# Moving attention side work between the units of a fused attention, rational-MLP and SoLU kernel

## The chip, the cores and the metric

The kernel runs on one core of one Trainium2 chip. The metric is the device time of one execution in microseconds (us), as the median of several runs. A profile is one further execution, recorded by the hardware profiler, with its own time.

## The reference

Three stages follow each other on 4 sequences of 768 tokens, with 8 heads of 48 (model width 384). What the kernel computes, cut to the core:

```python
# attention: a gated linear recurrence, state 48 x 48 for each head
state = alpha[:, :, t, :, None] * state + einsum('bhd,bhe->bhde', k[:, :, t], v[:, :, t])
y[:, :, t] = einsum('bhd,bhde->bhe', q[:, :, t], state)
x = y as (3072 tokens, 384)
# first feed-forward, 384 -> 2048 -> 384, a rational function in between
h = x @ w_in
g = (a[0] + a[1] * h + a[2] * h**2 + a[3] * h**3) / (1 + |b[0]| * |h| + |b[1]| * h**2 + 1e-6)
x = g @ w_out
# second feed-forward, 384 -> 1024 -> 384
h = x @ w_in2
ln = layer_norm(h * softmax(h)) * g_ln
out = ln @ w_out2
```

The weights come in 64-bit words that are turned into float32 on the chip. Float32 products are made of three passes with operands split into a high and a low part (hi x hi, hi x lo, lo x hi).

## The kernel before

**Units and halves.** The 3072 tokens are cut into 6 chunks of 512, and the first feed-forward runs in 96 units: unit u works on chunk u // 16 and on columns 128 (u % 16) of the hidden layer. A unit has an up-projection `m_up` of 9 matmuls of 512 columns (L592) into one of three PSUM banks "h", and a chain of elementwise steps: on ScalarE abs L597, two squares L599 and L600, ln L619, exp L620 and the rounded high part gh L625; on VectorE L618, L621, L622, L623; on GpSimd the low part gl L626. The down-projection `m_down` of 9 matmuls (L638) follows four units later and adds up over a chunk's 16 units in three PSUM banks x2p. There is one set of these banks, so the first down-projection of a chunk waits until the copies of the last sums (x2e, L646 on ScalarE) have left them; SP then stores x2e (L647).

**Side work.** Eight units are a half, and beside each half runs the attention of one half chunk ahead (`half_steps`, L853): two generators are advanced by a step a unit. `a_pe` makes the scores in two parts (L420 on TensorE, copy L427 on ScalarE, causal mask L428 on GpSimd), then y (L444; high part L470 on ScalarE, low part L471 on VectorE), then the keys-values product u (L483; state updated on VectorE L493 and GpSimd L494). The preparation `a_dve` (transposes L290 to L337, the scan L317) runs for the half after, then moves of q and k, loads of alpha and k (L266) for the half after that, and at the end `a_enter`. Scores, y, u and the conversions below share a ring of two PSUM banks "at".

**Second weights.** The 14 tiles of the second feed-forward's weights are converted by `split_w` as side work, two tiles a half: load L533 into a buffer "st", three integer steps on VectorE (L537, L540, L541), a scale L546 (tiles of the second matrix alone) and a rounding copy L547 on ScalarE, a subtraction on GpSimd (L548), a store L550. The tag "st" has two buffers, which x2e and the output tiles o use too.

**Second phase.** From unit 80 the last chunk runs, and from unit 89 the second feed-forward's tiles of 128 tokens begin, 24 in all: `n_up` (18 matmuls, L712), softmax and norm `n_soft`, `n_norm` (L731 to L752), every four tiles a turn `n_turn` by 16 SP transfers (L762), `n_split` into high part (L767, ScalarE) and low part (L768, GpSimd, tiles 0 and 20 VectorE), `n_down` (24 matmuls, L776, two banks "op") and `n_out` (copy L785 on ScalarE, four stores L788 on SP). `SKIP` names the tiles s after which no `n_down` follows, so that as many are left for the tail behind the last `n_up`.

**What sets the order.** The program is written in the order of this loop; a list scheduler of the framework then orders each engine's instructions by its own costs, and `issue_after` keeps some of them behind a named instruction. On each engine and DMA queue instructions start in that order. Buffers of a ring are handed on when their last reader is done.

Of the kernel before, what the change touches and what calls it, by code (L numbers as in the profile page):

```python
# [30 lines left out]
def kernel(  # L31
# [17 lines left out]
    B, H, S, D = q.shape  # L49
# [7 lines left out]
    NF1 = DF1 // 128  # L57
# [20 lines left out]
    G2 = 3  # L78
    MIX = lambda u: u < 24 and u % 2 == 0
    EARLY = (9, 11, 13, 15)  # L80
    SKIP = (5, 7, 11)
    AHEAD = 3
    LATE = 2
    U2, IDLE = NF1 - 1, (0, NF1 // 2 - 1)
    assert (B, H, D, CH) == (4, 8, 48, 128)

    const = ctx.enter_context(tc.tile_pool(name="const", bufs=1, side="left"))
# [65 lines left out]
    def network(fast):  # L153
# [257 lines left out]
        def a_pe(i):  # L411
# [4 lines left out]
            for p in range(2):  # L416
                sc = [ps_ap.tile([128, B, CH], F32, name="sc", tag="at") for j in range(2)]
                for x in range(B):
                    for j in range(2):
                        nc.tensor.matmul(  # L420
                            sc[j][:, x, :],
                            lhsT=hf.k[p][64 * j:64 * j + D, x, :], rhs=hf.q[p][64 * j:64 * j + D, x, :],
                            start=True, stop=True,
                        )
                for j in range(2):
                    t = A[p, j] = ap_.tile([128, B, CH], F32, name="A", tag=f"A{p}{j}")
                    nc.scalar.activation(t, sc[j], AF.Copy)  # L427
                    nc.gpsimd.affine_select(  # L428
                        out=t, in_=t, pattern=[[0, B], [1, CH]], compare_op=ALU.is_ge, fill=0.0, base=0,
                        channel_multiplier=-1,  # L430
                    )
                yield
            end = ap_.tile([128, B, 2], F32, name="end", tag="end", bufs=2)
            nc.gpsimd.tensor_copy(end, hf.ends[:, :, :, 0])
            ends = _view(end[:], 0, [[2, B], [1, 2], [0, D]])
# [35 lines left out]
                marks[i, z] = nc.vector.tensor_tensor(lo, y2[z], hi.bitcast(F32), ALU.subtract)  # L471
            yield
            if i >= NPE:
                yield
            if i < NPE:
                a_back(i)
# [398 lines left out]
        for u in range(NU + LAG):  # L875
            c, f = divmod(u, NF1)
            now[0] = u
            if f % (NF1 // 2) == LATE and u < NU:
                _run(side)
                i = 2 * c + 2 + f // (NF1 // 2)  # L880
                side = half_steps(i) if fast and i < NH else iter(())
# [21 lines left out]
            if u == NU:  # L903
                _run(n_load(1))
            take(side, 1)
            if u >= U2 and f % (NF1 // 2) in IDLE:
                stage["bank"] = "at"
                with later(G2):
                    take(split2, 1)
# [18 lines left out]
        for s in range(len(EARLY), NS):  # L928
            if s % B == 0 and 1 < s // B + 1 < NCH:
                _run(n_load(s // B + 1))  # L930
            n_tile(s)
            if s % B == B - 1:
                n_turn(s // B)
            while cut < min(done + AHEAD, (s + 1) // B * B):
                n_split(cut)
# [124 lines left out]
```

## Time and profile before

| | us |
|---|---|
| median of 3 runs | 779.71 (774.92 to 781.45) |
| the profiled execution's own time | 776.87 |
| its span on the core | 775.0 |
| TensorE busy in the span | 728.0 (94%) |
| VectorE busy | 630.4 (81%) |
| ScalarE busy | 535.2 (69%) |
| GpSimd busy | 358.4 (46%) |

The span is what the profiler saw from the first to the last instruction, and 1.87 us of the execution lie around it. Busy time is the sum over the whole span; the kernel has stages with different limits, so the stages have to be read one by one. TensorE's granted clock was 0.972 of full speed in the mean.

### The profile page before, as it was taken

The numbers are of one execution on the slowest core, as the hardware profiler recorded it, in microseconds if no ns is written. First come the engines' busy times: TensorE is split into PE (matmuls) and PEld (weight loads), VectorE is DVE, ScalarE is ACT, GpSimd is POOL, SyncE is SP. The second block draws the span as 40 slices with busy tenths as digits, with TensorE's granted clock in tenths as the row PEclk, the third lists the DMA queues.
The fourth block names the chain that finished last, engine by engine and source line by source line (L and its number), as shares of the span: only waits on it lengthen the run. The fifth ranks groups of instructions, "written<-read, shape, count | busy, mean of one in ns | idle before, by whom it ended". The sixth has DMA issues, their size and how long they took to land.

```text
span 775.0 us, 13914 instructions
## 1 busy us (share of the span) xinstructions
PE 728.0 (94%) x4976; PEld 605.8 (78%) x4976; DVE 630.4 (81%) x1110; ACT 535.2 (69%) x983; POOL 358.4 (46%) x306
## 2 busy tenths in 40 slices
PE   4676999999999999999999999999999999999996
PEld 3565767788888787778877788888888989988986
DVE  4999999989898989899898966478887788877640
ACT  2245867689878888788878887788965545555541
POOL 3255777777554355434444433332243343452322
PEclk9857899999999999999999999999999999999999
DMA  7995446466837382727554350720025253542653
GB/s 167 253 275 165 107 155 167 146 147 206 204 99 161 122 205 83 172 66 207 137 148 91 124 82 1 296 112 0 1 83 132 89 130 90 132 108 52 140 119 76
DMA packets 87278, 101.74 MB, mean 131 GB/s; under 512 B 34464, under 2 KB 63136, under 8 KB 87200
## 3 DMA queue, kind: packets, MB, share of 16 engines
q1 hardware_dynamic: 87104, 100.67, 48.9%
q8 instruction: 41, 0.67, 0.4%
q14 instruction: 37, 0.30, 0.1%
q10 hardware_dynamic: 96, 0.10, 0.0%
HBM read 60.59 MB, written 27.56 MB: 114 GB/s over the span
## 4 chain that ended last, share of the span: by engine, by line
DVE 30%; PE 18%; ACT 12%; issue 5%; SPq 3%; DMA 3%; POOL 1%; ACTq 0%; DVEq 0%; POOLq 0%
PE x2p L638 6%; PE hp L592 6%; DVE room L752 3%; SPq L762 3%; DVE room L735 2%; DVE p L618 2%; ACT jk L737 2%; PE op L776 2%; DVE hp L622 2%; DVE w L621 2%; DMA room<-room 2%; DVE sm L731 2%; DVE room L750 2%; PE h L712 2%; DVE p L623 2%
## 5 line engine op out<-in xcount | busy, mean ns | idle before, releaser
L592 PE MATMUL hp<-xt,g 128*128 128x512 f32 x864 | 224.1, 401 | 14.8 <-DVE p L616 7.5
L626 POOL TENSOR_TENSOR gl<-p,gh 128x512 fp32r<-128x512 f32 x96 | 130.8, 1362 | 193.9 <-ACT gh L625 107.9
L592 PEld LDWEIGHTS hp<-xt,g 128*128 128x128 f32 x864 | 163.2, 192 | 54.2 <-DVE p L616 7.7
L638 PE MATMUL x2p<-gh,g 128*128 128x512 f32 x576 | 196.9, 395 | 2.0 <-ACT x2e L646 2.0
L638 PEld LDWEIGHTS x2p<-gh,g 128*128 128x128 f32 x576 | 107.9, 188 | 29.1 <-ACT x2e L646 4.7
L638 PE MATMUL x2p<-gl,g 128*128 128x512 f32 x288 | 112.9, 392 | 0.0
L776 PE MATMUL op<-w2oh,room 128*128 128x384 f32 x384 | 101.8, 339 | 1.3 <-ACT room L767 0.7
L768 POOL TENSOR_TENSOR room<-room,room 128x1024 fp32r<-128x1024 f32 x22 | 54.8, 2496 | 101.0 <-ACT room L767 79.0
L621 DVE SCALAR_TENSOR_TENSOR w<-w,co,hp 128x512 f32<-128x512 f32 x84 | 62.0, 738 | 43.5 <-ACT hp L620 42.5
L712 PE MATMUL h<-w2ih,x 128*128 128x512 f32 x288 | 90.7, 394 | 0.0
L599 ACT ACTIVATE p<-hp,co 128x512 f32<-128x512 f32 x96 | 66.0, 687 | 12.3 <-POOL gl L626 12.0
L620 ACT ACTIVATE hp<-ah 128x512 f32<-128x512 f32 x84 | 50.1, 597 | 33.3 <-DVE p L618 32.0
L776 PEld LDWEIGHTS op<-w2oh,room 128*128 128x128 f32 x384 | 70.1, 188 | 3.0 <-ACT room L767 1.0
L600 ACT ACTIVATE w<-ah,co 128x512 f32<-128x512 f32 x96 | 69.4, 724 | 1.7 <-DVE hp L622 1.3
L618 DVE SCALAR_TENSOR_TENSOR p<-p,co,hp 128x512 f32<-128x512 f32 x84 | 61.6, 734 | 9.3 <-ACT p L599 9.0
L597 ACT ACTIVATE ah<-hp 128x512 f32<-128x512 f32 x96 | 56.7, 591 | 16.4 <-PE hp L592 16.0
L776 PE MATMUL op<-w2ol,room 128*128 128x384 f32 x192 | 65.0, 339 | 0.0
L625 ACT ACTIVATE gh<-p 128x512 fp32r<-128x512 f32 x96 | 59.9, 623 | 5.7 <-DVE p L623 2.8
L638 PEld LDWEIGHTS x2p<-gl,g 128*128 128x128 f32 x288 | 54.1, 188 | 11.7 <-issue 0.8
L712 PEld LDWEIGHTS h<-w2ih,x 128*128 128x128 f32 x288 | 53.9, 188 | 11.7
L623 DVE SCALAR_TENSOR_TENSOR p<-p,co,hp 128x512 f32<-128x512 f32 x84 | 61.9, 737 | 1.1
L619 ACT ACTIVATE ah<-w,co 128x512 f32<-128x512 f32 x84 | 60.6, 721 | 1.3
(168 smaller groups left out, 1264.7 us busy)
## 6 DMA issues: line engine op xcount, KB each, us to landing
room<-room SPq DMA_DIRECT2D x96, 128.0 KB, 2.3
qk_d<-qk SPq DMA_DIRECT2D x10, 771.0 KB, 4.1
st<-in_moe_w_in_dram SPq DMA_DIRECT2D x13, 512.0 KB, 4.6
st<-in_moe_w_out_dram SPq DMA_DIRECT2D x16, 384.0 KB, 3.5
qks<-qk_d SPq DMA_DIRECT2D x20, 257.0 KB, 4.4
x<-x_d SPq DMA_DIRECT2D x18, 256.0 KB, 3.1
out_dram<-o SPq DMA_DIRECT2D x94, 48.0 KB, 1.6
ra<-in_alpha_dram SPq DMA_DIRECT2D x44, 96.0 KB, 2.8
```

The costliest lines, as they stand in the source:

```text
L592: last["PE", u] = nc.tensor.matmul(hp, lhsT=w[:, kt, 128 * o:128 * o + 128], rhs=xts[c][:, kt, xx, :], start=(kt == 0 and w is hi and xx = ...
L599: nc.scalar.activation(p, hp, AF.Square, bias=co[:, 7:8])
L600: nc.scalar.activation(w, ah, AF.Square, bias=co[:, 6:7])
L618: nc.vector.scalar_tensor_tensor(p, p, a1, hp, ALU.add, ALU.mult)
L619: nc.scalar.activation(ah, w, AF.Ln, bias=rest)
L621: nc.vector.scalar_tensor_tensor(w, w, rest, hp, ALU.add, ALU.mult)
L623: fin[u] = nc.vector.scalar_tensor_tensor(p, p, a0, hp, ALU.add, ALU.mult)
L625: last["ACT", u] = nc.scalar.activation(gh, p, AF.Copy)
L626: last["POOL", u] = nc.gpsimd.tensor_tensor(gl, p, gh[:].bitcast(F32), ALU.subtract)
L638: nc.tensor.matmul(x2ps[c][d], lhsT=w[:, o, 128 * d:128 * d + 128], rhs=gg, start=(f == 0 and w is hi and gg is gh), stop=(f == NF1 - 1 an ...
L712: nc.tensor.matmul(hp[:, 512 * n:512 * n + 512], lhsT=x2s[c][:, kt, x, CH * b:CH * b + CH], rhs=w2[w][:, kt, 512 * n:512 * n + 512], start ...
L776: nc.tensor.matmul(op, lhsT=x[:, 128 * f:128 * f + 128], rhs=w2[w][:, f, :], start=(f == 0 and x is hi and w == "oh"), stop=(f == NF2 - 1 ...
```

## The change

From unit 16 on, a half's side work starts at unit 1 of the half instead of unit 2, and a step is put in ahead of y and another ahead of u. So the two parts of the scores come with units 1 and 2 instead of 2 and 3, y stays at 4, u comes at 7 instead of 6, and the entering work falls on unit 0 of the next half. The second weights' conversion steps come at units 0 and 6 of a half instead of 0 and 7, after two first steps at units 15 and 16. `SKIP` gets tile 15, so one more `n_down` is left for the tail; and at every fourth tile the splits of tiles already turned are written ahead of the new turn.

```diff
-    SKIP = (5, 7, 11)
+    SKIP = (5, 7, 11, 15)
     AHEAD = 3
-    LATE = 2
-    U2, IDLE = NF1 - 1, (0, NF1 // 2 - 1)
+    LATE = lambda u: 2 if u < NF1 else 1
+    U2, IDLE = NF1 - 1, lambda u: (u + (u < NF1 + 4)) % (NF1 // 2) in ((0, 1) if u < NF1 + 4 else (0, 6))
...
                 yield
+            if i >= 2 * NPE:
+                yield
             end = ap_.tile([128, B, 2], F32, name="end", tag="end", bufs=2)
...
             yield
             if i >= NPE:
+                yield
+            if i >= 2 * NPE:
                 yield
             if i < NPE:
                 a_back(i)
...
-            if f % (NF1 // 2) == LATE and u < NU:
+            if f % (NF1 // 2) == LATE(u) and u < NU:
...
-            if u >= U2 and f % (NF1 // 2) in IDLE:
+            if u >= U2 and IDLE(u):
...
             n_tile(s)
             if s % B == B - 1:
+                while cut < min(done + AHEAD, s // B * B):
+                    n_split(cut)
+                    cut += 1
                 n_turn(s // B)
             while cut < min(done + AHEAD, (s + 1) // B * B):
                 n_split(cut)
```

Lines of the changed kernel are 2 to 7 higher (L592 is L596 there, L638 is L642, L444 is L446). In the fences below, up-projections write hp, down-projections x2p, with numbers that name the bank's tile.

On TensorE, around the border between the third and the fourth chunk (the up-projections of units 51 and 52, the last sums of chunk 2 in x2p_3028 and the first of chunk 3 in x2p_3981), before:

```order
L638 MATMUL x2p_3028<-gh,g_974 128x512
L592 MATMUL hp<-xt,g_629 128x512 x7
L420 MATMUL sc<-qks 128x128 x8
L592 MATMUL hp<-xt,g_629 128x512 x2
L638 MATMUL x2p_3981<-gh,g_134 128x512
L638 MATMUL x2p_3981<-gl,g_134 128x512
```

and after, with x2p_3037 and x2p_3990 in their places:

```order
L642 MATMUL x2p_3037<-gh,g_974 128x512
L596 MATMUL hp<-xt,g_629 128x512 x9
L446 MATMUL y<-qks,Sbd 32x128 x12
L446 MATMUL y<-A,vns 32x128 x16
L446 MATMUL y<-qks,Sbd 32x128 x12
L446 MATMUL y<-A,vns 32x128 x16
L642 MATMUL x2p_3990<-gh,g_134 128x512
```

The scores have left this place for the unit before, and y has come in between the last sums of one chunk and the first of the next.

On SP in the same half (rq, rk, ra are loads for the preparation, x_d_69 the stores of x2e, kb_d and qk_d results of the preparation), before:

```order
L266 DMA rk<-in_k_dram 32x4x192 x3
L647 DMA x_d_69<-x2e 128x1024
L266 DMA rk<-in_k_dram 32x4x192
L647 DMA x_d_69<-x2e 128x512
L329 DMA kb_d<-alT 128x768
L533 DMA st<-in_moe_w_out_dram 128x384
L266 DMA ra<-in_alpha_dram 32x4x192 x4
L533 DMA st<-in_moe_w_out_dram 128x384
```

and after:

```order
L266 DMA rk<-in_k_dram 32x4x192 x4
L329 DMA kb_d<-alT 128x768
L266 DMA ra<-in_alpha_dram 32x4x192 x3
L651 DMA x_d_69<-x2e 128x1024
L266 DMA ra<-in_alpha_dram 32x4x192
L651 DMA x_d_69<-x2e 128x512
L537 DMA st<-in_moe_w_out_dram 128x384
L337 DMA qk_d<-qk 128x3x514
L537 DMA st<-in_moe_w_out_dram 128x384
```

Both stores of x2e now stand between the loads ra and the loads st, and behind kb_d.

On VectorE in the same half (units 52 to 54; L621 takes the exponential of its unit), before:

```order
L621 SCALAR_TENSOR_TENSOR w<-w,co,hp 128x512
L471 TENSOR_TENSOR xt<-y,xt 128x2x256
L471 TENSOR_TENSOR xt<-y,xt 128x256
L622 SCALAR_TENSOR_TENSOR hp<-w,hp 128x512
L537 TENSOR_SCALAR fp<-st 128x384
L623 SCALAR_TENSOR_TENSOR p<-p,co,hp 128x512
L540 SCALAR_TENSOR_TENSOR fp<-st,fp 128x384
L541 SCALAR_TENSOR_TENSOR ft<-st,fp 128x384
L537 TENSOR_SCALAR fp<-st 128x384
L618 SCALAR_TENSOR_TENSOR p<-p,co,hp 128x512
```

and after:

```order
L473 TENSOR_TENSOR xt<-y,xt 128x2x256
L473 TENSOR_TENSOR xt<-y,xt 128x256
L541 TENSOR_SCALAR fp<-st 128x384
L544 SCALAR_TENSOR_TENSOR fp<-st,fp 128x384
L622 SCALAR_TENSOR_TENSOR p<-p,co,hp 128x512
L545 SCALAR_TENSOR_TENSOR ft<-st,fp 128x384
L625 SCALAR_TENSOR_TENSOR w<-w,co,hp 128x512
L626 SCALAR_TENSOR_TENSOR hp<-w,hp 128x512
```

The three integer steps of the tile now stand between y's low part and the L625 (before L621) of the next unit; before, that unit's L621 stood ahead of them all.

At the end of the program on SP (room is a turn of four tiles, out_dram the output stores; the last two rows are the last turn and what is behind it), before:

```order
L762 DMA room_6225<-room_6208 32x1024 x16
L788 DMA out_dram<-o 32x384 x16
L762 DMA room_6225<-room_5889 32x1024 x16
L788 DMA out_dram<-o 32x384 x20
L762 DMA room_6225<-room_6208 32x1024 x16
L788 DMA out_dram<-o 32x384 x22
```

and after:

```order
L766 DMA room_6225<-room_6208 32x1024 x16
L792 DMA out_dram<-o 32x384 x12
L766 DMA room_6225<-room_5889 32x1024 x16
L792 DMA out_dram<-o 32x384 x19
L766 DMA room_6225<-room_6208 32x1024 x16
L792 DMA out_dram<-o 32x384 x27
```

Of the 96 stores, four a tile and two on ScalarE's queue, 22 stood behind the last turn and 27 do now; tile 16 has three of its four ahead of the turn.

On ScalarE at the end (room_6352 is a tile's high part, o its output copy), before:

```order
L746 ACTIVATE sm<-sm 128x1
L785 ACTIVATE o<-op 128x384 x2
L767 ACTIVATE room_6352<-room_6225 128x1024
L785 ACTIVATE o<-op 128x384
L767 ACTIVATE room_6352<-room_6225 128x1024 x3
L785 ACTIVATE o<-op 128x384 x4
```

and after:

```order
L750 ACTIVATE sm<-sm 128x1
L771 ACTIVATE room_6352<-room_6225 128x1024
L789 ACTIVATE o<-op 128x384 x2
L771 ACTIVATE room_6352<-room_6225 128x1024 x3
L789 ACTIVATE o<-op 128x384 x2
L771 ACTIVATE room_6352<-room_6225 128x1024
L789 ACTIVATE o<-op 128x384 x4
```

Before, the copies of tiles 17 to 19 stand ahead of the high parts of tiles 21 to 23; after, those of tiles 18 and 19 stand behind the high parts of tiles 20 to 22.

## Rows read from the trace of the kernel before

**Rows 1.** Halves: bounds, length, busy PE, PEld, DVE, ACT, POOL, clock, DMA, GB/s.

```profile
240.28:281.80 41.52, 40.70 (x321) 32.49 (x320) 37.92 (x63) 34.42 (x63) 17.66 (x17) 1.00 0.52 148
281.80:324.04 42.24, 40.80 (x322) 32.71 (x321) 39.15 (x65) 34.29 (x64) 21.28 (x19) 1.00 0.58 141
324.04:365.98 41.94, 41.14 (x322) 32.34 (x321) 37.39 (x61) 35.74 (x66) 17.86 (x18) 1.00 0.51 144
365.98:407.96 41.98, 40.78 (x321) 32.73 (x320) 38.87 (x65) 34.05 (x63) 21.17 (x19) 1.00 0.59 142
407.96:450.21 42.25, 41.20 (x322) 32.36 (x320) 35.82 (x59) 36.00 (x66) 18.79 (x18) 1.00 0.43 112
450.21:490.25 40.04, 40.04 (x322) 32.67 (x320) 25.97 (x38) 32.73 (x57) 13.11 (x14) 1.00 0.20 37
```

**Rows 2.** Waits of PEld in 324.04 to 365.98: total us, times, longest.

```profile
PEld x2p L638 <- ACT x2e L646: 1.6, 2, 0.9
```

**Rows 3.** Waits of PEld in 281.80 to 324.04.

```profile
PEld u L483 <- DVE xt L471: 1.1, 1, 1.1
PEld y L444 <- POOL A L428: 0.8, 1, 0.8
```

**Rows 4.** Waits of DVE in 281.80 to 324.04.

```profile
DVE w L621 <- ACT hp L620: 2.4, 3, 0.9
```

**Rows 5.** Timeline of PEld, 304 to 312 us: start, length, instruction, idle time before.

```profile
304.65 2.00 PEld L592 LDWEIGHTS hp<-xt,g 128*128 128x128 f32 x9
...
307.23 0.60 PEld L444 LDWEIGHTS y<-qks,Sbd 128*32 128x32 f32 x24 [0.35 <-ACT ah L597]
...
311.40 0.19 PEld L638 LDWEIGHTS x2p<-gl,g 128*128 128x128 f32 x1 [0.20 <-issue]
```

**Rows 6.** Costliest groups of ACT by line: busy us, mean ns, idle before.

```profile
L620 ACT ACTIVATE hp<-ah 128x512 f32<-128x512 f32 x84 | 50.1, 597 | 33.3 <-DVE p L618 32.0 <-ACT gh L625 0.4
L546 ACT ACTIVATE ft<-ft,gln 128x384 f32<-128x384 f32 x8 | 4.9, 613 | 4.0 <-DVE ft L541 3.9
```

**Rows 7.** Timeline of SP's queue at 352 us.

```profile
352.59 0.38 SPq L533 DMA_DIRECT2D st<-in_moe_w_out_dram  x1
353.27 1.83 SPq L266 DMA_DIRECT2D ra<-in_alpha_dram  x4
```

**Rows 8.** Timeline of DVE, 352 to 362 us.

```profile
352.52 0.72 DVE L290 STREAM_TRANSPOSE qk<-rq 128x256 f32<-128x256 f32 x1
...
361.71 0.55 DVE L537 TENSOR_SCALAR fp<-st 128x384 int32<-128x384 int32 x1
```

**Rows 9.** DMA issues of the page: KB each, median us to landing.

```profile
out_dram<-o SPq DMA_DIRECT2D x94, 48.0 KB, 1.6
...
x_d<-x2e SPq DMA_DIRECT2D x6, 512.0 KB, 3.1
```

**Rows 10.** Line L533 alone, all its loads.

```profile
DMA to landing us min/median/max: 2.8/4.7/10.0
```

**Rows 11.** Masks and scan: timelines of POOL and DVE, and L317 by line.

```profile
301.03 0.64 POOL L428 TENSOR_SCALAR_AFFINE_SELECT A<-A 128x512 f32<-128x512 f32 x1 [0.90 <-ACT A L427]
306.19 2.85 POOL L428 TENSOR_SCALAR_AFFINE_SELECT A<-A 128x512 f32<-128x512 f32 x2 [0.68 <-ACT A L427]
...
304.67 2.45 DVE L317 TENSOR_TENSOR_SCAN alT<-alT,d 128x774 f32<-128x774 f32 x1
...
L317 DVE TENSOR_TENSOR_SCAN alT<-alT,d 128x774 f32<-128x774 f32 x10 | 19.3, 1928 | 0.0
```

**Rows 12.** Timelines of SP's queue, PE and ACT in the tail.

```profile
745.25 10.87 SPq L762 DMA_DIRECT2D room<-room  x16
...
750.60 0.45 PE L776 MATMUL op<-w2oh,room 128*128 128x384 f32 x1 [0.71 <-ACT room L767]
...
751.86 0.62 PE L776 MATMUL op<-w2oh,room 128*128 128x384 f32 x2 [0.64 <-DVE room L768]
...
768.81 0.49 ACT L785 ACTIVATE o<-op 128x384 f32<-128x384 f32 x1 [3.74 <-PE op L776]
```

## The prediction

> **What bounds the kernel now.** I read the page first, then the stretches of eight units side by side, then what PE and VectorE waited for in them, then single places in the timeline. The page has TensorE busy for by far the largest share of the span, so what a reordering can win is what PE loses. The table of stretches shows where. Each row runs from the first up-projection matmul of a half (units 32, 40, 48, 56, 64, 72) to that of the next. The half that starts at 450.21 has no preparation and no conversion beside its units, and takes 40.04 us; I call that the PE floor, since the PE work of all these halves is the same. The five halves before it take 41.52, 42.24, 41.94, 41.98 and 42.25 us, 209.93 together (450.21 less 240.28) against 5 x 40.04 = 200.2 [rows 1]. So the steady part of the kernel holds 9.7 us of lost PE time, and this is the most that moving the side work can give there. The granted clock is 1.00 in all six, so no clock is to be won. Earlier units are placed as before, and from unit 80 on PE is full again up to the last tiles.
>
> Whose wait is it? In a half with a chunk's border (the stretches from 240.28, 324.04, 407.96) PE waits 1.6 us in two pieces for the copies of the down-projection sums to leave their only banks (x2e, L646) [rows 2]. In the others it waits 1.1 us at the keys-values product for VectorE's L471 and 0.8 us at y for GpSimd's masks (L428) [rows 3]. These are positions in a row, not lack of an engine. But VectorE is close behind: in the half from 281.80 it is busy 39.15 us of 42.24 [rows 1] and waits another 2.4 us for ScalarE's exponential [rows 4], which leaves 0.7 us of small gaps. Busy time plus gaps is 39.85, under the PE floor by 0.2 us. Whatever the change adds to VectorE's waits comes out at PE.
>
> **The change part by part.**
>
> *Scores, y and u moved.* In the order of the changed kernel the second scores come a unit earlier, y stands straight behind a whole unit's up-projection, and u behind a whole unit instead of behind one matmul of it. At the border the x2e copies now have an up-projection and y to hide behind: an up-projection takes 2.0 us (304.65) and y 3.3 (from 307.23 to 311.40 [rows 5], less the wait in it), 5.3 us, where before they had an up-projection and 16 short score matmuls, about 3 us. The copies came 1.6 us too late then; 5.3 covers that. For the masked scores of y the second scores are 5.2 us back (two matmuls, a down- and an up-projection of 2.0 us each, and y's first part, which needs no scores), for u its L471 a unit and more. So I let the waits of [rows 2] and [rows 3] go. If all of them and VectorE's lateness went, 9.7 us would be won; if none, nothing. The sum depends on what VectorE does next.
>
> *The conversion moved (last but one of each half, and first of the next).* It costs the same instructions, but lands elsewhere in VectorE's row: after the move the three integer steps of a tile stand directly ahead of the next unit's L621, and on ScalarE the scale (L546) of that tile stands between ln and exp of the unit that L621 waits for. So L621 now waits for one scale and one exponential in a row, 0.61 + 0.60 = 1.2 us [rows 6], once per half that has a conversion. Before, another unit's steps stood there. VectorE works ahead of PE by little, so I count it as added to VectorE's loop.
>
> *The load of the converted tile, in halves with a border.* The tile's buffer "st" is one of two that x2e also uses. Before, SP issued the x2e stores early and the load of the tile at 352.59, ahead of the four loads of 1.83 us [rows 7]; VectorE reached the first integer step only at 361.71, 9.1 us later [rows 8]. Now the order puts three of those loads, the first x2e store, the fourth load and the second store ahead of the load. Counted from the end of VectorE's last transpose (352.52 + 0.72 = 353.24): three loads 1.4 us, landing of the store, for whose buffer the load waits, 3.1 us [rows 9], so issue at +4.5; the load lands 2.8 to 10.0 us after its issue, 4.7 in the middle [rows 10], so at +9.2. VectorE gets there at about +7.3 (before +8.5; one elementwise step and part of a gap less stand ahead). The wait is 1.9 us by the middle, nothing if the load lands in 2.8, 7.2 if in 10.0. I take 1.5, a little under the middle, since that row counts the first matrix's larger tiles (512 KB) too. The Trainium skill ("DMA: Bandwidth & Descriptors", section "Anatomy of one DMA — SWDGE (gpsimd) path") gives 2.0 us plus bytes at 436 GB/s for a transfer on another queue than this one; taken for the x2e store (512 KB) and the load (384 KB) it makes 3.2 and 2.9 us, the load at +7.5 and the wait 0.2 us. The rows have 3.1 and 4.7, so only the store agrees.
>
> *Sum of the middle.* VectorE's loop in border halves: busy 37.92 and 37.39 (37.65 mean) + 0.7 + 1.2 + 1.5 = 41.05 us. In the two others: 39.15 and 38.87 (39.0) + 0.7 + 1.2 = 40.9, less 0.5 for a scan that took 2.45 us beside the masks, against a mean of 1.93 [rows 11], and has another neighbour now: 40.4. The half from 407.96 has no conversion: PE floor and a little, 40.3. Together 41.05 + 40.4 + 41.05 + 40.4 + 40.3 = 203.2, against 209.93: **6.7 us won** (0 to 9.7).
>
> *The tail.* With one more tile held back, PE's work ahead of the product of tile 20 is the same, so holding back gives PE nothing by itself; it only brings the last tile's chain forward by one product, 4.2 us (the last four products take from 751.86 to the copy at 768.81) [rows 12]. Before, the last turn (16 transfers, 10.87 us of issue) started at 745.25, and product 20 lost 0.71 and 0.64 us to it [rows 12]: 1.4 us is what the tail can give. But in the changed order the fourth store of tile 16 stands on SP behind the whole last turn, tile 18's output copy waits for it (two "st" buffers), and product 20 waits for that copy (two banks). The turn can start at 745.25 - 4.2 = 741.0; the store is issued at 741.0 + 10.9 = 751.9, lands 1.6 us later [rows 9], the copy takes 0.5: product 20 starts at 754.0 instead of 751.86. **2.1 us lost** (from 1.4 won, if the order hurts nobody, to 6.3 lost, if the last chain doesn't move and the turn starts at 745.25). Behind product 20 the end is the same.
>
> *Entering at 0, the split ahead of the turn, the loads of the second phase.* The first two are issues and copies on engines with room there, and I cost them at nothing: ACT is at 34 to 36 us of 42 [rows 1]. The first loads of the second phase (L677) stand ahead of the second weights' loads in the changed order, behind them before; I see no one waiting for that and cost it at nothing too. If one of them landed in 10.0 us like the slowest tile load [rows 10], the first tile's ScalarE copies and PE behind them would lose part of 5 us; that lies inside the upper end.
>
> Sum on the profiled execution: 776.87 - 6.7 + 2.1 = 772.3. Its time is 2.84 below the median of 779.71; on the scale of medians **775.1 us**, 0.6% faster.
>
> **The rivals.**
>
> *All of it is won.* VectorE's two new waits fall into time in which it would have waited anyway (its 2.4 us for the exponential [rows 4] overlap with them), and the tail's order hurts nobody: -9.7 - 1.4 = -11.1, 768.6 us. For it: in the half from 240.28 PE lost only 1.5 us, as much as x2e alone. Against: busy and gaps alone are at the floor.
>
> *The masks' wait moves along.* GpSimd's two masks took 2.85 us beside VectorE's scan and the product behind it, where a mask alone takes 0.64 [rows 11]. If they meet the scan again, each stands behind one VectorE instruction, up to 2.75 us for both and 1.3 of their own, after copies that end 2 us behind the scores: 6.1 us, over the 5.2 us of cover, and y waits 0.85 us as it did. Five halves: 4.2 us back, 779.4. The Trainium skill ("SBUF — State Buffer", section "SBUF: two separate sides") says that VectorE with two SBUF inputs and GpSimd hold a shared port pair exclusively, the later one blocking; 2.85 us for two masks fits that. Against: preparation moved too, but by its own steps.
>
> *The load of the converted tile is late: slower.* If the loads behind the x2e stores land in 10.0 us, as the slowest did [rows 10], VectorE stands 7.2 us at the first integer step in both border halves, 5.7 more than I count: -4.6 + 11.4 = +6.8, 786.5. It decides from a landing of 6.6 us (wait 3.8 us, 2 x 2.3 over my count, the whole gain). For it: the load shares the rings with the four loads and the stores just ahead of it. Against: 10.0 is the slowest of all the loads at L533, and the middle one is 4.7.
>
> *The last turn stays where it is.* The chain of the last tile hangs on ScalarE and VectorE, not on PE's up-projection: the tail loses 6.3, the middle wins 6.7, 779.3.
>
> **How the numbers follow.** My sum 0.47 (own range 772 to 779), all won 0.16, masks 0.14, last turn 0.11, late load 0.12. The time is that of the sum. The range goes from the full gain, 768.0, to between the neutral cases and the late load, 783.0, and leaves out most of the late load and a little below. One per cent, about what a measurement of this kernel can tell from no change, is 7.8 us: faster means under 771.9, which takes all of the full gain and some of the sum's lower side, 0.25; slower means over 787.5, about half of the late load, and what I have not seen, 0.11; the rest is 0.64.
>
> **What would show it.** Right: PE's waits for x2e, for L428 at y and for L471 at u are gone between units 32 and 72; halves of 40.3 to 41.1 us, longer ones at the borders, with VectorE waiting there for the load at the first integer step and everywhere 1.2 us at L621 behind a scale; product 20 about 2 us later against the end of product 19 than before, ScalarE waiting for the fourth store of tile 16. Wrong: halves at 40.1 (full gain), y waiting for L428 again, VectorE waiting over 3.8 us for the load, or a stall of more than 5 us ahead of product 20. A new wait where the second phase opens would be outside all of it.

## The result, and the profile after

The changed kernel takes 789.18 us (median of 6 runs, 786.25 to 790.1), the kernel before 778.89 beside it (6 runs): a ratio of 1.0145, 95% interval 1.0117 to 1.0174. The forecast was 775.1 with a range of 768 to 783: the time lies outside it, on the other side. The profiled execution of the changed kernel took 786.25 us with a span of 784.4; the span before was 775.0, so the spans differ by 9.4 us.

The span splits where orders can be compared. Up to unit 24 the changed kernel is 1.35 us ahead (198.69 against 200.04); that isn't the change, since the orders are the same up to about unit 16 and the profiles of all kernels below reach unit 24 between 196.7 and 201.3 us. From unit 24 to unit 72 it loses 3.25 us (253.42 against 250.17), the half from 72 is the same to 0.01 us, and from unit 80 to the end it loses 7.5 us (784.4 - 492.15 = 292.25 against 775.0 - 490.25 = 284.75). So both parts lost, and the tail lost more.

The halves after, first row from unit 24, the next six from unit 32 on as in [rows 1], same columns:

```profile
198.69:240.73 42.04, 41.13 (x321) 32.89 (x320) 39.59 (x63) 33.35 (x61) 23.11 (x20) 1.00 0.59 160
240.73:282.66 41.93, 40.93 (x321) 32.53 (x319) 37.88 (x61) 33.88 (x62) 19.35 (x19) 1.00 0.48 138
282.66:325.40 42.74, 41.44 (x320) 32.68 (x321) 40.28 (x65) 34.93 (x65) 20.84 (x19) 1.00 0.58 146
325.40:367.24 41.84, 41.02 (x322) 32.64 (x321) 38.58 (x61) 34.82 (x64) 19.02 (x19) 1.00 0.51 138
367.24:409.81 42.57, 41.32 (x321) 32.58 (x321) 40.11 (x65) 34.74 (x65) 20.66 (x19) 1.00 0.57 144
409.81:452.11 42.30, 40.81 (x321) 32.65 (x320) 38.95 (x63) 36.06 (x66) 18.01 (x18) 1.00 0.41 108
452.11:492.15 40.04, 40.04 (x321) 32.68 (x320) 25.22 (x36) 32.33 (x56) 12.85 (x13) 1.00 0.15 33
```

Not one half between 24 and 72 came near the floor of 40.04. VectorE's busy time (the third with a count) is what grew: 40.28 and 40.11 where it had 39.15 and 38.87, in halves in which it was idle for 3.1 us before.

What PE waited for in the half from 282.66, against [rows 3]:

```profile
PEld hp L596 <- DVE p L627: 2.3, 3, 0.9
PEld x2p L642 <- ACT gh L629: 0.7, 1, 0.7
PEld y L446 <- POOL A L428: 0.7, 1, 0.7
```

The wait for L471 at u is gone, and in the border halves those for x2e too, as the change is written to do. In their place an up-projection waits for VectorE's last step L627 on the PSUM bank it needs (hp), a down-projection waits for the high part gh, and y still waits for the masks. VectorE's own waits, in the border half from 240.73, against [rows 4]:

```profile
DVE fp L541 <- DMA st<-in_moe_w_out_dram: 2.0, 1, 2.0
DVE w L625 <- ACT hp L624: 1.2, 1, 1.2
```

These are the two waits that the prediction added, at about the sizes it gave. In the border half from 325.40 the load's one is 1.2 us. What it didn't have is this, from the timelines of GpSimd and of VectorE around 302 us, against [rows 11]:

```profile
299.39 1.22 POOL L428 TENSOR_SCALAR_AFFINE_SELECT A<-A 128x512 f32<-128x512 f32 x2
302.30 1.30 POOL L630 TENSOR_TENSOR gl<-p,gh 128x512 fp32r<-128x512 f32 x1 [1.69 <-ACT gh L629]
304.26 2.81 POOL L428 TENSOR_SCALAR_AFFINE_SELECT A<-A 128x512 f32<-128x512 f32 x2 [0.67 <-ACT A L427]
...
299.98 0.66 DVE L313 TENSOR_SCALAR qk<-P 128x6 f32<-128x6 f32 x1 [0.18 <-ACT jk L236]
...
302.59 2.62 DVE L317 TENSOR_TENSOR_SCAN alT<-alT,d 128x774 f32<-128x774 f32 x1
```

The low part gl starts 0.29 us ahead of the scan L317, and the scan takes 2.62 us instead of 1.75; the small L313 takes 0.66 beside the first masks; the second masks, issued while the scan runs, take 2.81 instead of 2 x 0.64. Before, the scan was stretched in two halves from unit 16 on (2.45 and 2.47 us). Now it is so in all seven of them, the first three of the ten scans lying ahead of it:

```profile
L317 DVE TENSOR_TENSOR_SCAN alT<-alT,d x10: 1765/2609/2625, 59.4 to 428.7; 128x774 f32<-128x774 f32 x10
```

(ns, least, median and most of the ten). The tail, on SP's queue, ScalarE and PE, against [rows 12]:

```profile
745.44 10.15 SPq L766 DMA_DIRECT2D room<-room  x16
755.64 23.40 SPq L792 DMA_DIRECT2D out_dram<-o  x27
...
758.05 0.49 ACT L789 ACTIVATE o<-op 128x384 f32<-128x384 f32 x1 [1.80 <-DMA out_dram<-o]
...
758.60 0.69 PE L780 MATMUL op<-w2oh,room 128*128 128x384 f32 x1 [5.81 <-ACT o L789]
```

Here is the chain that the order showed: the last turn, behind it the fourth store of tile 16, then the copy of tile 18 that waits for its buffer, then product 20. PE stands 5.81 us. And what follows costs too; the stretches before, during and after that wait, with the granted clock behind the five engines' times:

```profile
738.00:752.00 14.00, 13.52 (x76) 12.87 (x75) 6.54 (x13) 5.85 (x11) 5.06 (x2) 1.00 0.45 105
752.63:758.60 5.97, 0.16 (x2) 0.01 (x1) 0.00 (x0) 2.27 (x3) 4.61 (x2) 0.77 0.78 179
758.60:762.90 4.30, 4.30 (x14) 4.30 (x15) 0.00 (x0) 0.49 (x1) 0.07 (x1) 0.52 0.37 93
762.90:768.00 5.10, 5.10 (x31) 5.10 (x30) 0.00 (x0) 1.44 (x2) 2.06 (x1) 1.00 0.13 32
```

After nearly 6 us of idleness the granted clock is 0.52, the lower of its two levels (1.2 GHz), for 4.3 us. In the stretch behind it three matmuls start every 0.53 us, 177 ns each; at that pace the 14 of the slow stretch would have taken 2.5 us, so some 2 us more are lost.

### The profile page after: what moved, and what is told of

Its sections match the earlier page's. It is cut to its first block, busy times and chain, and to the rows that moved or that the text cites. A ratio compares the mean times of both kernels' runs of the same rounds, so it can differ in the third digit from the quotient of the medians.

```text
span 784.4 us, 13952 instructions
## 1 busy us (share of the span) xinstructions
PE 733.4 (93%) x4976; PEld 609.4 (78%) x4976; DVE 637.3 (81%) x1110; ACT 535.1 (68%) x983; POOL 361.1 (46%) x306
## 4 chain that ended last, share of the span: by engine, by line
DVE 38%; PE 26%; DMA 12%; ACT 11%; issue 7%; SPq 6%; POOL 0%; DVEq 0%; ACTq 0%; POOLq 0%
PE hp L596 10%; PE x2p L642 10%; SPq L766 4%; DMA st<-in_moe_w_out_dram 3%; DVE room L756 3%; PE op L780 2%; DVE room L739 2%; ACT jk L741 2%; DVE p L622 2%; DVE w L625 2%; DVE qk L290 2%; DVE alT L324 2%; DVE sm L735 2%; DVE hp L626 2%; SPq L266 2%
## 5 line engine op out<-in xcount | busy, mean ns | idle before, releaser
L596 PE MATMUL hp<-xt,g 128*128 128x512 f32 x864 | 222.6, 400 | 17.5 <-DVE p L620 8.1
L630 POOL TENSOR_TENSOR gl<-p,gh 128x512 fp32r<-128x512 f32 x96 | 128.8, 1342 | 180.9 <-ACT gh L629 140.0
L596 PEld LDWEIGHTS hp<-xt,g 128*128 128x128 f32 x864 | 162.5, 191 | 58.8 <-DVE p L627 11.4
L642 PE MATMUL x2p<-gh,g 128*128 128x512 f32 x576 | 195.6, 396 | 0.6 <-ACT gh L629 0.6
L642 PEld LDWEIGHTS x2p<-gh,g 128*128 128x128 f32 x576 | 108.6, 189 | 25.8 <-ACT gh L629 1.4
L642 PE MATMUL x2p<-gl,g 128*128 128x512 f32 x288 | 114.0, 396 | 0.0
L780 PE MATMUL op<-w2oh,room 128*128 128x384 f32 x384 | 103.5, 343 | 6.3 <-ACT o L789 6.2
L625 DVE SCALAR_TENSOR_TENSOR w<-w,co,hp 128x512 f32<-128x512 f32 x84 | 62.3, 742 | 35.5 <-ACT hp L624 33.5
L642 PEld LDWEIGHTS x2p<-gl,g 128*128 128x128 f32 x288 | 54.5, 189 | 12.5 <-issue 0.8
L627 DVE SCALAR_TENSOR_TENSOR p<-p,co,hp 128x512 f32<-128x512 f32 x84 | 62.3, 742 | 1.4
```

The source lines that it names most:

```text
L596: last["PE", u] = nc.tensor.matmul(hp, lhsT=w[:, kt, 128 * o:128 * o + 128], rhs=xts[c][:, kt, xx, :], start=(kt == 0 and w is hi and xx = ...
L625: nc.vector.scalar_tensor_tensor(w, w, rest, hp, ALU.add, ALU.mult)
L627: fin[u] = nc.vector.scalar_tensor_tensor(p, p, a0, hp, ALU.add, ALU.mult)
L630: last["POOL", u] = nc.gpsimd.tensor_tensor(gl, p, gh[:].bitcast(F32), ALU.subtract)
L642: nc.tensor.matmul(x2ps[c][d], lhsT=w[:, o, 128 * d:128 * d + 128], rhs=gg, start=(f == 0 and w is hi and gg is gh), stop=(f == NF1 - 1 an ...
L780: nc.tensor.matmul(op, lhsT=x[:, 128 * f:128 * f + 128], rhs=w2[w][:, f, :], start=(f == 0 and x is hi and w == "oh"), stop=(f == NF2 - 1 ...
```

## The experiments

The kernels were compared with the kernel before on the same chip. "24 to 72" is the time in the profile from the first up-projection matmul of unit 24 to that of unit 72, "from 80" that from unit 80 to the end of the span.

| kernel | median us | before, us | ratio, 95% interval | 24 to 72 | from 80 |
|---|---|---|---|---|---|
| before | | 778.89 | 1 | 250.17 | 284.75 |
| the change | 789.18 | 778.89 | 1.0145 (1.0117 to 1.0174) | 253.42 | 292.25 |
| tail alone | 783.52 | 777.45 | 1.0074 (1.0050 to 1.0099) | 250.03 | 290.73 |
| change without tail | 780.94 | 777.45 | 1.0050 (1.0025 to 1.0075) | 253.92 | 285.24 |
| side work alone | 773.78 | 777.45 | 0.9946 (0.9922 to 0.9970) | 245.58 | 284.14 |
| conversion alone | 778.53 | 777.45 | 1.0006 (0.9981 to 1.0032) | 250.04 | 285.00 |
| tail, stores moved | 778.05 | 778.13 | 0.9995 (0.9971 to 1.0019) | 250.28 | 284.40 |
| tile 15 in SKIP alone | 797.97 | 778.13 | 1.0252 (1.0214 to 1.0290) | 250.25 | 307.65 |
| change without tail, no masks | 774.18 | 778.13 | 0.9946 (0.9927 to 0.9965) | 250.01 | 284.27 |
| earlier start alone | 774.26 | 778.13 | 0.9957 (0.9934 to 0.9980) | 248.17 | 284.33 |
| the change, stores moved | 779.90 | 778.46 | 1.0024 (0.9998 to 1.0050) | 253.70 | 283.89 |
| side work alone, no masks | 766.55 | 778.46 | 0.9852 (0.9825 to 0.9878) | 242.11 | 284.81 |
| side work, u at 6 | 772.32 | 778.46 | 0.9921 (0.9892 to 0.9949) | 242.39 | 289.48 |
| side work, y at 3, u at 6 | 774.87 | 778.48 | 0.9973 (0.9948 to 0.9997) | 246.95 | 284.20 |
| side work, u at 6, tail with stores moved | 772.28 | 778.57 | 0.9921 (0.9895 to 0.9948) | 244.78 | 285.76 |

**The theory.** T: the tail's loss is the store queue (6 to 7 us), and the middle's loss is VectorE's time: the named waits do go, but the side work at its new place collides with GpSimd, which fills the slack that was to cover the moved conversion. T's rivals: M, that the tail is late only because the middle hands over late; and, for the middle, that the conversion's place alone costs it.

**The tail alone.** On the kernel before:

```diff
-    SKIP = (5, 7, 11)
+    SKIP = (5, 7, 11, 15)
...
             if s % B == B - 1:
+                while cut < min(done + AHEAD, s // B * B):
+                    n_split(cut)
+                    cut += 1
                 n_turn(s // B)
```

> The kernel before with the change's tail alone: tile 15 in SKIP and the splits of turned tiles ahead of the turn; side work and conversion as before. Theory T (in the tail the output copy of tile 18 waits for the fourth store of tile 16, which SP issues behind the whole last turn, so product 20 starts about 6 us late and runs its first microseconds at the lower clock): 7 to 8 us over the kernel before, about 786.5; PE stands 5.5 to 6.5 us ahead of product 20, and the half lengths up to unit 80 are those of before. Theory M (the tail only looks late because the middle handed its tiles over late): within 2 us of the kernel before.

Measured 1.0074, 6.1 us. The middle is that of before (250.03), the loss lies behind unit 80, and PE's wait ahead of product 20 is there, in PE's timeline:

```profile
754.27 0.69 PE L776 MATMUL op<-w2oh,room 128*128 128x384 f32 x1 [5.77 <-ACT o L785]
```

M falls for this loss; 6.1 is a little less than T said.

**The change without its tail.** On the changed kernel:

```diff
-    SKIP = (5, 7, 11, 15)
+    SKIP = (5, 7, 11)
...
             if s % B == B - 1:
-                while cut < min(done + AHEAD, s // B * B):
-                    n_split(cut)
-                    cut += 1
                 n_turn(s // B)
```

> The change without its tail: side work from unit 1, steps ahead of y and u, conversion at 0 and 6; SKIP and the splits as before. Theory T: the middle costs 1 to 4 us net, since VectorE's loop is the bound in every half (1.2 us behind a scale, 1 to 2 us for the load at borders, scans of 2.6 us beside GpSimd), so 780 to 783; halves of 41.8 to 42.8 us from unit 24 on. Theory M: 785 or more, all of the loss is in the middle.

Measured 1.0050, 3.5 us: in T's range. Tail and middle add up, 0.74% and 0.50% to 1.45% within the intervals.

**Side work alone, and conversion alone.** Both on the kernel before. The first has the changed `LATE` and the two added steps, and nothing else:

```diff
-    LATE = 2
+    LATE = lambda u: 2 if u < NF1 else 1
...
+            if i >= 2 * NPE:
+                yield
             end = ap_.tile([128, B, 2], F32, name="end", tag="end", bufs=2)
...
             if i >= NPE:
                 yield
+            if i >= 2 * NPE:
+                yield
             if i < NPE:
```

The second has the changed `IDLE` alone:

```diff
-    U2, IDLE = NF1 - 1, (0, NF1 // 2 - 1)
+    U2, IDLE = NF1 - 1, lambda u: (u + (u < NF1 + 4)) % (NF1 // 2) in ((0, 1) if u < NF1 + 4 else (0, 6))
```

> Only scores, y, u and the preparation moved; conversion at units 0 and 7 and the tail as before. If the moved conversion is what fills VectorE (1.2 us behind a scale each half, the load at borders), this gains against the full middle: halves of 40.5 to 41.5, 2 to 5 us under the kernel before. If it is the scans and masks side by side with GpSimd, which move with the side work, this stays at 0 to 3 us over the kernel before, with y still waiting 0.7 to 0.9 us for the masks and the scan L317 at 2.6 us.

> Only the conversion moved to units 0 and 6 (15 and 16 first); side work and tail as before. If the conversion's place costs 1.2 us a half and the load at the borders: 3 to 6 us over the kernel before, and PE's waits for x2e and for L471 at u stay. If its place costs nothing: within 1 us of the kernel before.

The side work alone wins 0.54% (24 to 72: 4.6 us less). The conversion alone does nothing, and the order says why: with the side work at its old place the scheduler puts every instruction of the five engines in the same row as before, and a few DMAs of SP change places. So this run is no test of the new place; only beside the moved side work does the conversion move at all, and there it loses: 253.92 against 245.58, 8.3 us. The expectation for the side work had two branches, and both are half true. It gains, but less than it could, and with the signs of the second branch: the scan is at 2.6 us and y waits for the masks four times, 1.9 us in all. GpSimd's low part and VectorE's scan in it:

```profile
299.97 1.30 POOL L630 TENSOR_TENSOR gl<-p,gh 128x512 fp32r<-128x512 f32 x1 [1.68 <-ACT gh L629]
...
300.28 2.62 DVE L317 TENSOR_TENSOR_SCAN alT<-alT,d 128x774 f32<-128x774 f32 x1
```

**The tail with the stores on another queue.** On the kernel with the tail's edit alone:

```diff
-                (nc.scalar if s == NCH * B - 1 and b >= 2 else nc.sync).dma_start(out=to[b], in_=o[32 * b:32 * b + 32])
+                (nc.scalar if s in (16, 17) or s == NCH * B - 1 and b >= 2 else nc.sync).dma_start(out=to[b], in_=o[32 * b:32 * b + 32])
```

> The tail's edit alone, with the eight stores of tiles 16 and 17 issued from ScalarE's queue instead of SP's; the instructions are else the same. If the late product 20 comes from those stores standing behind the last turn on SP, PE's stall ahead of it falls from about 6 us to 1 to 2.5 us, the clock stays up, and the time is that of the kernel before, 776 to 779. If it comes from the last turn itself or from the order on ScalarE, the stall stays at 5 us or more and the time at 783 to 784.

Measured 0.9995: the whole loss is gone, and the stretch from unit 80 is 284.40. PE doesn't wait ahead of product 20 at all; the longest wait of the tail is 0.77 us for a copy. The same turn, started within 0.6 us of the same place, hurts nobody when the stores of two tiles don't stand behind it, so the turn is not the cause. But the edit doesn't win anything either. And it changed more than the queue: the scheduler also put the copies of tiles 18 and 19 back ahead of the high parts of tiles 21 and 22 on ScalarE, where the changed kernel has them behind that of tile 22. ScalarE with the high part of tile 20 and the copy of tile 18:

```profile
749.60 1.06 ACT L767 ACTIVATE room<-room 128x1024 fp32r<-128x1024 f32 x1 [3.81 <-DMA out_dram<-o]
750.57 0.47 ACT L785 ACTIVATE o<-op 128x384 f32<-128x384 f32 x1
```

In the changed kernel the copy of tile 18 found ScalarE free and waited another 1.80 us for the store (the row at 758.05 above). That part of PE's 5.81 us is the store's alone; in the rest the copy stood behind the high parts. The edit of the queue removes both, and how much ScalarE's order would cost without the late stores isn't shown.

**Tile 15 in SKIP alone.** The split ahead of the turn is left out.

```diff
-    SKIP = (5, 7, 11)
+    SKIP = (5, 7, 11, 15)
```

> Tile 15 in SKIP alone, the splits left behind the turn. 34 stores stand behind the last turn in this order, so tiles 15 to 17 wait for it as well: a stall ahead of product 19 or 20 of 6 us or more, 783 to 788. If the split ahead of the turn is what makes the stall, this is within 2 us of the kernel before.

1.0252, 20 us: worse than expected, but of the kind. Two waits for a high part, of 6.33 us and 8.89 us, stand ahead of products 13 and 17, not 19 or 20, each with a granted clock of 0.50 behind it, and 34 stores are behind the last turn. With the split ahead of the turn, in the run of the tail alone, the loss was 6.1 us.

**The change without its tail and without masks.**

```diff
-                    nc.gpsimd.affine_select(
+                    if i < 2 * NPE:
+                        nc.gpsimd.affine_select(
...
```

> The change without its tail, and without the causal masks (L428) from the fifth half on: GpSimd's affine selects are left out, so y there takes unmasked scores. If GpSimd's masks are what stretches the scan L317 to 2.6 us, it falls to 1.75 and VectorE wins 0.9 us a half beside the 0.5 us of L313: 5 to 8 us under the change without its tail (780.9). If the low part gl stretches the scan, L317 stays at 2.6, only L313 falls from 0.66 to 0.17 and y's wait goes: 2 to 5 us under it, because VectorE still sets the halves.

774.18, 6.8 us under the change without its tail, or 1.04% by the two ratios. The scan is at 1.76 and L313 at 0.17 in every half, so the first branch by its numbers. But the reason it gives is not the one in the rows: here too a low part gl runs beside the scan, 2.68 us long, only that it starts 0.17 us behind the scan and not 0.3 ahead. It is the order of the two starts that decides who is stretched; leaving the masks out moved that order. (The profiled execution was the slowest of the twelve, with a wait of 3.03 us for a load in one half, so its 24 to 72 shows less than the median.)

**Side work alone without masks.** The same edit on the side work alone.

> The side work moved alone, conversion and tail as before, and without the causal masks (L428) from the fifth half on, so y there takes unmasked scores. If GpSimd's meeting with VectorE is what kept the side work from the full 9.7 us, the halves from unit 32 to 72 fall from 205.3 to 201 to 203 us and the time to 769 to 772. If VectorE's instructions fill the halves anyway, they stay at 204 or more and the time at 773 to 775.

766.55: below the range that was expected. Five of the six halves from unit 24 on take 40.04 to 40.27 us, the floor; one takes 41.68. VectorE's scan and GpSimd's low part in it:

```profile
297.67 1.77 DVE L317 TENSOR_TENSOR_SCAN alT<-alT,d 128x774 f32<-128x774 f32 x1
297.86 2.67 POOL L631 TENSOR_TENSOR gl<-p,gh 128x512 fp32r<-128x512 f32 x1 [2.84 <-DVE p L623]
```

So without the masks the side work's move is worth 8.1 us from unit 24 to 72, nearly all of the 9.9 that these six halves held over the floor. With them it is worth 4.6. Leaving the masks out takes away the collisions and y's wait for the masks together, so what each of the two is worth isn't shown.

Four of the kernels make a table of their own: side work moved, with and without the masks, with and without the moved conversion. The moved conversion costs 8.3 us from 24 to 72 with the masks (245.58 to 253.92) and 7.9 us without them (242.11 to 250.01), 1.04% and 0.94% by the medians' ratios. The masks with their collisions cost 3.5 us without the moved conversion and 3.9 us with it. So the two losses add up, and T is wrong in one point: the conversion costs as much where the scan takes 1.76 us, so the stretched scan is not what makes it dear. For the middle the rival holds as far as this: beside the moved side work the conversion's place costs by itself.

**The earlier start, and one step at a time.** Three kernels have the changed `LATE` with none, the first or the second of the two added steps, the conversion and the tail as before. The first added step is

```diff
                 yield
+            if i >= 2 * NPE:
+                yield
             end = ap_.tile([128, B, 2], F32, name="end", tag="end", bufs=2)
```

and stands ahead of y; the second, ahead of u, has the same two lines.

> Only the start of the halves moved to unit 1, without the two added steps: scores at 1 and 2, y at 3, u at 5; conversion and tail as before. If the early second scores and preparation are what wins, this is at 773 to 775 like the side work moved as a whole. If y behind a whole unit and u at 7 matter, x2e and L471 are waited for again and it is at 777 to 780.

> The side work moved without the step ahead of u: scores at 1 and 2, y at 4, u at 6; conversion and tail as before. If u at 7 matters for its wait on L471, that wait is back at 0.4 to 1.1 us a half and the time is 775 to 778; if the gain is that of the earlier scores with y left at 4, it is 772 to 775 as with both steps.

> The side work moved without the step ahead of y: scores at 1 and 2, y at 3, u at 6; conversion and tail as before. If the step ahead of u is what brings VectorE's scan and GpSimd's low part into each other's way, the scan L317 takes about 2.6 us in most halves here too, and the halves from unit 32 to 72 stay at 204 to 208 us (773 to 776). If it takes both added steps to do it, the scan stays at 1.75 and the halves fall to 201 to 203 us (771 to 773).

With none, 0.9957: the time is that of the first branch, the waits are those of the second. Two halves are at 43.45 and 42.76 us, and u waits for L471 twice, 2.7 us; the others are at 40.06 to 40.85. With y alone put back to 4 and u at 6: 0.9921, and the halves take 40.04 to 40.90 us; the wait for L471 is not back (0.35 us twice). With y at 3 and u at 6: 0.9973, scan at 1.75 to 1.83, and yet 246.95 from 24 to 72, where 201 to 203 for the five halves was expected and 206.55 came: VectorE waits 2.06 us three times for ScalarE's exponential. That expectation missed. Both kernels with a single step have no stretched scan from unit 24 on, so it takes both steps together to bring scan and low part into that order in every half. An unstretched scan isn't enough for a gain, as the kernel with y at 3 shows; the one with y at 4 alone gains most. In its timelines the low part is just done:

```profile
296.95 1.30 POOL L628 TENSOR_TENSOR gl<-p,gh 128x512 fp32r<-128x512 f32 x1 [1.25 <-ACT gh L627]
...
298.30 1.77 DVE L317 TENSOR_TENSOR_SCAN alT<-alT,d 128x774 f32<-128x774 f32 x1
```

From unit 80 on this kernel takes 289.48 us, 4.7 more than before, though on VectorE, ScalarE and GpSimd the order is that of before from 60 us behind unit 80 on. Its last turn starts 257.3 us behind unit 80 (255.0 before), and PE waits 2.65 us for a high part. Why that turn is late wasn't settled; the other kernels with the old tail take 284.1 to 285.3 us.

**The whole change with the stores moved.**

On the changed kernel:

```diff
-                (nc.scalar if s == NCH * B - 1 and b >= 2 else nc.sync).dma_start(out=to[b], in_=o[32 * b:32 * b + 32])
+                (nc.scalar if s in (16, 17) or s == NCH * B - 1 and b >= 2 else nc.sync).dma_start(out=to[b], in_=o[32 * b:32 * b + 32])
```

> The changed kernel as a whole, with the eight stores of tiles 16 and 17 on ScalarE's queue. If middle and tail add up without touching each other, the tail's 6 us go and what is left is the change without its tail: 780 to 783, 0.3 to 0.7% over the kernel before. If the two hang together, 785 or more.

1.0024, 779.9, at the lower edge of what was expected: the tail's loss is gone and the middle's is left (253.70 from 24 to 72). They add up.

**The best of both.** Side work with u at 6, conversion as before, the tail's edit with the stores on ScalarE's queue; on the kernel of the last diff:

```diff
-    U2, IDLE = NF1 - 1, lambda u: (u + (u < NF1 + 4)) % (NF1 // 2) in ((0, 1) if u < NF1 + 4 else (0, 6))
+    U2, IDLE = NF1 - 1, (0, NF1 // 2 - 1)
...
             if i >= NPE:
                 yield
-            if i >= 2 * NPE:
-                yield
             if i < NPE:
```

> The side work without the step ahead of u (as in the run with y alone moved back to 4), the conversion as before, and the tail's edit with the stores of tiles 16 and 17 on ScalarE's queue. In the run without the tail's edit PE lost 4.7 us after unit 80 to the last turn's tile 20. If holding back tile 15 is worth something once the store queue is out of the way, those go and the stretch after unit 80 is 284 to 285.5 us, the time 766 to 770. If the last turn is late whatever is held back, the stretch stays at 288 or more and the time at 772.

772.28: the stretch from unit 80 falls from 289.48 to 285.76, near the 284 to 285.5 hoped for, but the time is that of the other branch and not better than without the tail's edit (772.32). In its profile unit 24 comes 1.6 us later, and from 24 to 72 it takes 2.4 us more, most of it in one half of 42.25 us. Why that half is long wasn't settled. 772.3 us, 0.8% under the kernel before, is the best that a version with all of the computation gave.

## Why the prediction was wrong

*What bounds the kernel.* Right: 9.7 us were there, and a kernel that leaves the masks out reached the floor in five of six halves. Of the signs of being wrong that I had named, two came: y waits for L428 again, and PE stands more than 5 us ahead of product 20.

*Scores, y and u moved.* The waits for x2e and for L471 went, as said; the wait for the masks did not. It stood among the rivals with 0.14: y waits 0.7 to 1.0 us in five of six halves, 4.1 us in all between units 24 and 72.

*The conversion moved: the first step that failed.* The waits came in place and size: 1.17 us at L621 behind a scale and an exponential, load issued 4.4 us after the last transpose (predicted 4.5), waits of 2.0 and 1.2 us (predicted 1.5). Wrong is what the move costs. "It costs the same instructions", I wrote, and the sum let most of the 7.8 us of waits fall into VectorE's slack, so that the five halves from unit 32 came to 203.2, 3.0 us over the floor's 200.2. They took 211.4: 41.9 and 41.8 us where 41.05 was said, 42.7 and 42.6 for 40.4, and 42.3 for 40.3. The moved conversion alone costs PE 8.3 us from 24 to 72 beside the moved side work, and 7.9 without the masks. That 8.3 is near 7.8 is luck, for most of it isn't those waits: a wait of 1.1 to 1.2 us behind the exponential is in every half with the side work alone too, and over units 16 to 79 VectorE's waits rose by 2.2 us only. The rest are longer instructions (2.5, of which the other scan, L308, is 1.9), lost overlap (2.4, below) and small gaps (1.2). These are readings of the two traces; an experiment that takes one of them away alone wasn't made. Nor was x2e tried with buffers of its own, for which there is no room.

*Sum of the middle: the second step that failed.* It read "less 0.5 for a scan that took 2.45 us beside the masks ... and has another neighbour now". The neighbour was the wrong one and the sign too. In the kernel before, GpSimd's row just ahead of that scan (at 304.67, [rows 11]) is

```profile
304.21 1.29 POOL L626 TENSOR_TENSOR gl<-p,gh 128x512 fp32r<-128x512 f32 x1 [2.54 <-issue]
```

The low part gl had started 0.46 us ahead of the scan, and the masks only came at 306.19. At the new place gl is ahead in every half: the scan takes 2.61 against 1.75, L313 0.66 beside the first masks against 0.17. With L308, at 2.18 against 1.75 in four halves, and L320 these lines of VectorE take 7.6 us longer over units 16 to 79 (L317 4.5, L313 3.0, L308 1.8, L320 1.7 less). In the halves that the sum put at 40.4 VectorE is busy 40.2 where the sum had 38.5. Without the masks 3.5 to 3.9 us of it came back from 24 to 72, y's wait for them included. I had the scan's row and put its length down to the masks, instead of asking which instruction had started first and who would start first at the new place.

*The tail: the mechanism right, the size not.* Product 20 began 6.1 us later than before against unit 80 (758.60 - 492.15 against 750.60 - 490.25). I had put it at 754.0 instead of 751.86, 2.1 us late; but 751.86 is the product's third matmul, behind its second wait, and against its first at 750.60 the same sum gives 3.4. The term that failed behind that is the turn's start: it moved 1.7 us forward, not 4.2 (745.44 - 492.15 = 253.3 against 255.0). Holding a tile back moves the last up-projection by a product, but between it and the turn lie softmax and norm on VectorE and ScalarE, and the last transpose of the norm (L752) ended only 1.7 us earlier against unit 80. From the turn's end to the copy it took 2.46 us, not 1.6, and the turn itself 0.7 less. And the slow clock behind the wait, some 2 us, was not in the sum: I read the granted clock as 1.00 and didn't ask what a longer idle time would do to it. The rival with the turn at its old place priced the wait alone at 6.3.

*The rivals.* The slower case that I wrote, a load of 10 us, did not come; three losses that I had each put down as small or nothing (the moved conversion, the masks with their collisions, the tail) came together, all on the same side. Masks and last turn had been weighed as if only one of them could happen.

*The rule of the Trainium skill* on the shared port ("SBUF — State Buffer", section "SBUF: two separate sides") was weighed for the masks alone. These runs agree with it: the later of the two waits, and the longer instruction is by about as much longer as the other had left to run (2.62 = 1.75 + 1.0 of gl, less 0.1; before, 2.45 = 1.75 + 0.8, less 0.1). It holds for gl and the scan as much as for masks, and gl is on GpSimd 64 times between units 16 and 79.

## What to carry to other kernels

When side work is moved against a fixed unit, look at every pair of instructions that then run side by side on VectorE and GpSimd, and ask which starts first; a shift of half a microsecond decides whether 0.9 us or more falls on the engine that has slack or on the one that has none. Slack of a second engine is to be read after the move, not before it: here the same instructions at another place in VectorE's row cost PE 8 us, most of it not in the waits that had been counted. And a store queue that shares its engine with a long series of transfers is part of a buffer's life; count what stands behind the series before changing what is held back.

## What the runs showed of the hardware

Which of two instructions is stretched depends on the order of the starts. With gl 0.19 us behind the scan (side work alone, no masks), gl takes 2.67 us and the scan 1.77; with gl 0.29 us ahead (the changed kernel), gl takes 1.30 and the scan 2.62. In both cases the second ends 2.9 us after the first began.

Neighbours on VectorE cost more if one needs the other's result. In the changed kernel, VectorE's timeline:

```profile
282.52 0.56 DVE L541 TENSOR_SCALAR fp<-st 128x384 int32<-128x384 int32 x1
283.12 0.56 DVE L544 SCALAR_TENSOR_TENSOR fp<-st,fp 128x384 int32<-128x384 int32 x1
283.59 0.74 DVE L625 SCALAR_TENSOR_TENSOR w<-w,co,hp 128x512 f32<-128x512 f32 x1
```

L544 needs L541's result and starts 0.04 us after its end; L625 needs nothing of L544 and starts 0.09 us ahead of its end. With the side work moved, moving the conversion too takes the instructions of units 16 to 79 that start over 0.04 us ahead of the end of the one before from 303 to 273 of 462. Their durations rose by 2.5 us in sum (322.39 to 324.93), but VectorE's busy time rose by 5.0, since 2.4 us of overlap were lost.

TensorE's granted clock fell from 1.00 to the lower level while it stood still for 5.8 us (0.77 in the mean of that stretch), and 4.3 us of work passed at 0.52 before it was back at 1.00; the price of a wait at the end is the wait and this.
